# A delta-rule attention with two MoE layers on one core: the sign of the decoded weights by a 32-bit step on VectorE, unread products in TensorE's early gaps, seven half buffers for the second decoding

## The chip, the core and the metric

The kernel runs on 1 core of one Trainium2 chip. The time is the device time of that core in microseconds (us), given as the median of three runs. The engines are called as in the profile: PE is TensorE (PEld its weight loads), DVE is VectorE, ACT is ScalarE, POOL is GpSimd, SP is the engine that issues the transfers.

## What is computed

The reference, cut to what matters (`_attn_ref`, then two MoE layers; each tells one layer's work):

```
k_n = k / (norm(k) + 1e-6)                     # q, k, v: [4, 8, 768, 48] float32
for t in range(768):
    y[:, :, t] = q[:, :, t] @ state            # state: [4, 8, 48, 48]
    v_old = k_n[:, :, t] @ state
    state += beta[:, :, t] * outer(k_n[:, :, t], v[:, :, t] - v_old)
x = y.transpose(0, 2, 1, 3).reshape(3072, 384)
x = (silu(x @ w_gate) * (x @ w_val)) @ w_out   # d_ff 1536
h = x @ w_in                                   # d_ff 2048
return where(h > 0, h, exp(min(h, 0)) - 1) @ w_out2
```

The weights of both MoE layers are float64. The kernel gets their bits as pairs of 32-bit words. The result is not read from the state after the last token.

## The kernel before

**Work and stages.** The 3,072 tokens are cut into 12 groups g of 256: 128 positions of two batches. For each group `prepare` loads q, k and v, normalises k, transposes q and k, forms the products of keys with keys and queries (L451), masks them into `gr` (L457, DVE, four instructions a group) and calls `invert`. That transposes the masked blocks into `ain` (L486), inverts a triangular matrix per 32 positions in small DVE steps (L501, L508) and, for groups 0 and 1, does this blocked: two halves of 16 (`halves`), joined by two sets of 64 small products on TensorE (`join1` L546, `join2` L560) with a step on DVE between them (`mid`). `attention` applies the inverse (L602), forms for every 32 positions a matrix that carries the state onward (L622), copies it with ACT and adds the queries to it (`plus`, L635, DVE, four instructions for each pair of batch and parity), and takes the state through the four pieces (`chain`: products on TensorE, L652, and two sums on DVE, L658, for each piece and batch). The output is read off all states at once, transposed and split into `xh` and `xl`, a rounded half and the difference (L755 and the others below do the same with weights). Every large fp32 product is done as three passes of such halves.

**First MoE** (`moe1`). Per group 12 blocks f of 128 hidden units: two projections of 9 products of 256 columns each (L832), Silu on ACT (L839), the product on DVE (L842), a rounded copy on ACT (L846), the difference on POOL (L849), and 12 output products into the accumulator `acc` (L857), which takes two banks. The groups' results go out to DRAM (`x2d`). **Second MoE** (`moe2`): six groups n of 512 tokens, 16 steps f each: 9 products of 512 columns (L942), three ACT passes, three DVE passes, 12 output products (L979).

**Decoding of weights** (`decode`). Each tile of 128 x 768 weights, 18 for the first MoE and 16 for the second, passes six steps: ACT scales the low word (`lowbits`, L755), ACT writes the magnitude of the high word into a temporary (`mag`, L761), the sign is put into the low word's top byte (on POOL with a compare, L768, or on DVE with a mask of bytes, L771; the planner chooses), DVE merges temporary and low word (`both`, L776), ACT copies the rounded half (`hi`, L786) and POOL forms the difference (`lo`, L790). The second decoding has three temporaries (the tiles `gr`, `st` and `dt`, which the attention no longer needs then), so three weights are under way at a time.

**What sets the order.** Class `Order` plans the whole program as a list of steps with costs, priorities and the buffers that they hold, and takes at every moment the ready step with the best priority (a smaller number goes first; on engines other than TensorE a step may be waited for during 0.35 of the chosen one's cost). What it yields is each engine's fixed order. Decoding of the first weights has priority 12 and above, between the attention of group 0 and that of group 1.

```
o_ = acc[:, d // 2, (d % 2) * TB:(d % 2) * TB + TB]            # moe1, prod
add(p, [("POOL", 1900.0, 1900.0, 0, sign(G)), ("DVE", 1350.0, 1430.0, 0, sign(V))],
    r=[key, keyb], w=[(key, "lo")])
add(p, [("DVE", 1110.0, 1170.0, 0, both)], r=[(key, "lo")], w=tkeys)
decode(n, tag, tk, att_pri(0) + 2 + 0.1 * n)                    # first decoding
```

Of the kernel before, what the change touches and what calls it, by code (L numbers as in the profile page):

```python
# [10 lines left out]
F16 = mybir.dt.float16  # L11
# [34 lines left out]
class Order:  # L46
# [41 lines left out]
    def run(self):  # L88
# [22 lines left out]
        while left:  # L111
# [23 lines left out]
            t, o, (e, occ, lat, k, f) = pick  # L135
            ready.remove(o)
# [34 lines left out]
def delta_moe_kernel(ctx: ExitStack, tc: tile.TileContext, q, k, v, beta,  # L171
# [12 lines left out]
    BLOCKED = (0, 1)  # L184
    JOIN = (2, 4, 5)
    LOPOOL = tuple(range(12))
    HIDVE = False
    DIFDVE = False
# [19 lines left out]
    ident = T("ident", [128, 128])  # L208
    strict = T("strict", [128, 32])
# [86 lines left out]
    def consts():  # L296
# [25 lines left out]
        for r0, r1 in ((32, 64), (64, 96)):  # L322
            for x, n, key in ((st, B * H, "st"), (sv, 2 * (C - 1) * H, "sv")):
                def f(x=x, n=n, r0=r0, r1=r1):
                    w_ = x[r0:r1].rearrange("p b (h d) -> p b h d", d=D) if x is st else \
                        x[r0:r1].rearrange("p a c (h d) -> p (a c) h d", d=D)
                    G.tensor_copy(out=w_.rearrange("p b h d -> p (b h) d"),
                           in_=ident[r0:r1, D:2 * D].unsqueeze(1).to_broadcast([32, n, D]))
                add(20, pool(n * D, f), r=["ident"] + (["stz"] if x is st else []),
# [248 lines left out]
    def attention(g, p):  # L578
# [32 lines left out]
        for a in range(2):  # L611
            for par in range(2):
# [14 lines left out]
                for c in range(C):  # L627
# [93 lines left out]
        batch(p, 4, [chain(0, C - 1), chain(1, C - 1)], g > 0)  # L721
# [18 lines left out]
    def decode(n, tag, tkeys, p):  # L740
# [23 lines left out]
        def sign(e):  # L764
            def f():
                by = buf[n].bitcast(U8).rearrange("p a (n b) -> p a n b", b=8)
                if e is G:
                    e.tensor_scalar(out=by[:, :, :, 3], in0=by[:, :, :, 7], scalar1=128.0,  # L768
                                    scalar2=128.0, op0=ALU.is_ge, op1=ALU.mult)
                else:  # L770
                    e.tensor_scalar(out=by[:, :, :, 3], in0=by[:, :, :, 7], scalar1=128, scalar2=None,  # L771
# [302 lines left out]
```

## Time and profile before

| | before |
|---|---|
| median of three runs | 1219.83 us (1219.39 to 1221.9) |
| the profiled execution | 1217.5 us |
| its span | 1215.8 us |
| PE busy | 1126.8 us, 93% |
| DVE busy | 807.2 us, 66% |
| ACT busy | 555.4 us, 46% |
| POOL busy | 281.0 us, 23% |

The span is the time from the first to the last instruction that the trace holds; the profiled execution takes 1.7 us more. The share of busy time is a mean over stages that differ much, so the table only tells which engine the whole leans on. Which wait ends last in a stage is to be read from that stage.

### The profile page before, as it was taken

How to read it: one execution, taken by the hardware profiler on the slowest of the kernel's cores; microseconds unless marked ns; L12 is line 12 of the kernel's file. 1: busy time of each engine (PE TensorE's matmuls, PEld its weight loads, DVE VectorE, ACT ScalarE, POOL GpSimd, SP SyncE). 2: the span in 40 equal slices, each digit the busy share in tenths (PEclk: the TensorE clock that was granted, in tenths of full speed). 3: DMA queues.
4: the chain of work that ended last, by engine and by line, in shares of the span. 5: the costliest groups of instructions: out<-in, count | busy, mean ns of one | idle time of the engine just before them, and what ended most of it. 6: DMA issues, size and time to landing. Idle time of an engine off the chain costs nothing.

```text
span 1215.8 us, 33783 instructions
## 1 busy us (share of the span) xinstructions
PE 1126.8 (93%) x14366; PEld 1042.5 (86%) x14366; DVE 807.2 (66%) x2485; ACT 555.4 (46%) x1098; POOL 281.0 (23%) x252
## 2 busy tenths in 40 slices
PE   2487789999999999999999999979999999999998
PEld 2477779989998999899899999868888888888887
DVE  7888577968787887869687731977544445454443
ACT  5574424243433435252424333876545545454543
POOL 6896112122121212121221112782000000000000
PEclk9979879999999999999999999989999999999998
DMA  9720111120202011120201002910100101010000
GB/s 289 203 73 14 29 28 27 29 41 16 42 16 41 22 35 31 26 49 7 55 2 30 2 15 89 334 63 18 52 10 2 52 1 52 1 35 1 26 1 27
DMA packets 106824, 57.32 MB, mean 47 GB/s; under 512 B 76944, under 2 KB 101520, under 8 KB 106672
## 3 DMA queue, kind: packets, MB, share of 16 engines
q1 hardware_dynamic: 106672, 55.16, 16.9%
q8 instruction: 112, 1.84, 0.6%
q14 instruction: 40, 0.33, 0.1%
HBM read 45.71 MB, written 9.44 MB: 45 GB/s over the span
## 4 chain that ended last, share of the span: by engine, by line
PE 74%; DVE 9%; issue 2%; POOL 1%; ACT 1%; DMA 1%; ACTq 0%; DVEq 0%; POOLq 0%
PE gv L832 19%; PE acc L857 9%; PE acc L979 8%; PE at L979 8%; PE at L942 8%; PE gv L942 8%; PE at L622 3%; PE at L652 3%; DVE ain L501 3%; DVE z L508 3%; PE at L602 2%; PE at L425 2%; PE at L675 2%; PE at L451 2%; DVE tb L842 1%
## 5 line engine op out<-in xcount | busy, mean ns | idle before, releaser
L832 PE MATMUL gv<-xh,w 128*128 128x256 f32 x1728 | 288.7, 287 | 7.3 <-ACT tb L839 4.8
L832 PEld LDWEIGHTS gv<-xh,w 128*128 128x128 f32 x1728 | 239.8, 192 | 11.6 <-ACT tb L839 5.6
L849 POOL TENSOR_TENSOR hb<-tb,hb 128x256 fp32r<-128x256 f32 x144 | 116.0, 805 | 397.7 <-ACT hb L846 346.7
L857 PE MATMUL acc<-hb,w 128*128 128x256 f32 x1296 | 186.1, 287 | 7.7 <-POOL hb L849 3.8
L857 PEld LDWEIGHTS acc<-hb,w 128*128 128x128 f32 x1296 | 166.4, 192 | 12.8 <-POOL hb L849 5.3
L832 PE MATMUL gv<-xl,w 128*128 128x256 f32 x864 | 151.0, 284 | 0.0
L839 ACT ACTIVATE tb<-gv 128x256 f32<-128x256 f32 x144 | 55.3, 384 | 200.4 <-PE gv L832 191.6
L501 DVE TENSOR_TENSOR ain<-z,ain 128x60 f32<-128x60 f32 (+22 forms) x580 | 123.8, 250 | 1.3
L832 PEld LDWEIGHTS gv<-xl,w 128*128 128x128 f32 x864 | 124.6, 192 | 0.0
L846 ACT CAST hb<-tb 128x256 fp32r<-128x256 f32 x144 | 58.5, 406 | 113.6 <-DVE tb L842 112.4
L842 DVE TENSOR_TENSOR tb<-gv,tb 128x256 f32<-128x256 f32 x144 | 61.1, 424 | 66.2 <-ACT tb L839 54.2
L508 DVE TENSOR_TENSOR z<-z,ain 128x60 f32<-128x60 f32 (+22 forms) x580 | 103.4, 217 | 1.4
L957 DVE SCALAR_TENSOR_TENSOR hb<-gv,hb 128x512 f32<-128x512 f32 x48 | 33.2, 692 | 95.3 <-ACT hb L954 95.3
L957 DVE SCALAR_TENSOR_TENSOR hb<-at,hb 128x512 f32<-128x512 f32 x48 | 33.2, 692 | 87.5 <-ACT hb L954 87.4
L948 ACT ACTIVATE hb<-gv 128x512 f32<-128x512 f32 x48 | 28.7, 599 | 94.6 <-PE gv L942 94.2
L954 ACT ACTIVATE hb<-hb,neg 128x512 f32<-128x512 f32 x96 | 69.5, 724 | 3.0
L948 ACT ACTIVATE hb<-at 128x512 f32<-128x512 f32 x48 | 28.7, 598 | 83.5 <-PE at L942 83.5
L951 ACT ACTIVATE hb<-hb 128x512 f32<-128x512 f32 x96 | 60.7, 633 | 3.0
L622 PE MATMUL at<-gr,R 32*96 32x80 f32 x1536 | 56.7, 264 | 4.0 <-DVE lc L635 3.0
L622 PEld LDWEIGHTS at<-gr,R 32*96 32x96 f32 x1536 | 48.0, 169 | 11.7 <-DVE lc L635 3.6
L658 DVE TENSOR_TENSOR sv<-at,sv 48x192 f32<-48x192 f32 x96 | 34.1, 355 | 31.4 <-PE at L652 29.2
L979 PE MATMUL acc<-w,kp 128*128 128x384 f32 x192 | 41.1, 347 | 6.2 <-DVE kp L962 4.4
(176 smaller groups left out, 2203.6 us busy)
## 6 DMA issues: line engine op xcount, KB each, us to landing
w<-in_moe_w_out_dram SPq DMA_DIRECT2D x28, 384.0 KB, 6.4
w<-in_moe_w_in_dram SPq DMA_DIRECT2D x16, 384.0 KB, 5.2
kp<-in_k_dram SPq DMA_DIRECT2D x12, 384.0 KB, 4.2
qp<-in_q_dram SPq DMA_DIRECT2D x12, 384.0 KB, 4.0
R<-in_v_dram SPq DMA_DIRECT2D x24, 192.0 KB, 2.8
w<-in_moe_w_gate_dram SPq DMA_DIRECT2D x12, 384.0 KB, 8.6
w<-in_moe_w_val_dram SPq DMA_DIRECT2D x12, 384.0 KB, 8.7
x2d<-hb SPq DMA_DIRECT2D x12, 256.0 KB, 2.0
```

What stands on the lines that cost most here:

```text
L501: V.tensor_tensor(out=t, in0=z[:, l:l + 1, x:y].to_broadcast([128, l, y - x]), in1=an[:, l, 0:l].unsqueeze(2).to_broadcast([128, l, y - x] ...
L508: V.tensor_tensor(out=z[:, 0:l, x:y], in0=z[:, 0:l, x:y], in1=t, op=ALU.add)
L622: PE.matmul(bank[h[c].got[0]][0:96, s * 80:s * 80 + 80], lhsT=R[t, u, :], rhs=gr[t, u, 0:80], start=True, stop=True, skip_group_check=True)
L832: PE.matmul(dst, lhsT=wt[:, a_, kk * 128:(kk + 1) * 128], rhs=xx[:, kk, :], start=(n == 0), stop=(n == 3 * KD - 1))
L842: V.tensor_tensor(out=c['s'], in0=bank[h.got[0]][:, TB:2 * TB], in1=c['s'], op=ALU.mult)
L849: return lambda: e.tensor_tensor(out=c['h'][:, 1, :], in0=c['s'], in1=c['h'][:, 0, :].bitcast(F32), op=ALU.subtract)
L857: PE.matmul(o_, lhsT=w[:, a_, d * 128:(d + 1) * 128], rhs=c['h'][:, b_, :], start=(f == 0 and n == 0 and d != 1), stop=(f == F1 - 1 and n ...
L942: PE.matmul(x, lhsT=W[f][:, 0, a_, kk * 128:(kk + 1) * 128], rhs=x2[n][b_][:, kk, :], start=(m == 0), stop=(m == 3 * KD - 1))
L951: A.activation(out=c['r'], in_=c['r'], func=ACTF.Exp, scale=-1.0)
L954: A.activation(out=c['r'], in_=c['r'], func=ACTF.Identity, bias=neg1, scale=1.0)
L957: V.scalar_tensor_tensor(out=c['r'], in0=bank[h.got[0]], scalar=0.0, in1=c['r'], op0=ALU.max, op1=ALU.add)
L979: PE.matmul(o, lhsT=c['h'][:, b_, t * 128:(t + 1) * 128], rhs=W[f][:, 1][:, a_, :], start=(f == 0 and m == 0), stop=(f == F2 - 1 and m == 2))
```

## The change

- **Sign.** POOL's compare and DVE's mask of bytes go. In their place stands one 32-bit step on DVE (`sign32`: the high word with all but the top bit cleared, or-ed into the low word; it stands 22 times in the new order) or one half-word copy on ACT (`sign16`, 12 times).
- **Differences.** The difference of a decoding may now be done on DVE (29 times) or POOL (5 times); that of a block of the first MoE is always on DVE (144 times, POOL before).
- **Sums with the queries.** `plus` becomes one DVE instruction of 512 elements on data that ACT has copied to SBUF (48 in all) in place of four of 128 on PSUM (192).
- **States.** The copies that set up the states go from POOL to ACT. For the last two groups the update after the last piece is left out; nothing reads it (32 products and four sums of states a group).
- **Unread products.** `warm` and `fill` put products of a constant 128 x 128 identity into TensorE's order, 403 in all, where the planner sees a gap before its time of 150 us. They write into `acc[:, 1, 384:512]`, which no step reads before it is started anew.
- **Priorities.** The first decoding moves from priority 12 + 0.1n to 14.8 + 0.02n. Steps with priority 12 or more are waited for during 0.1 of a cost, before 0.35.
- **Second decoding.** Its temporaries are seven half buffers (two each in the tiles `gr`, `st` and `dt`, one in `l2`), before three whole tiles.

```diff
+                    w = c[0] + (self.WAIT if c[1].pri[0] < 12 else 0.1) * c[2][1]
...
+            if e == "PE" and self.fill and t < self.until and left > 1:
+                gap = t - free.get("PE", 0.0)
+                n = int(self.share * gap / self.unit)
+                if n > 1:
+                    self.fill(n)
+                    kind[0] = k
...
+                def plus(a=a, par=par):
+                    b = 64 * par
+                    x = buf['lc', a][par][0:D, :, :, D:80]
+                    V.tensor_tensor(out=x, in0=x, in1=kq[b:b + D, a, :, 0, :].rearrange(
+                        "p j (c t) -> p j c t", c=C), op=ALU.add)
+                add(p, dve(512, plus), r=[("kq", a, 0)] + lk[a], w=[("lc", a, par, c) for c in range(C)])
...
-        batch(p, 4, [chain(0, C - 1), chain(1, C - 1)], g > 0)
+        if g // 2 < NI - 1:
+            batch(p, 4, [chain(0, C - 1), chain(1, C - 1)], g > 0)
...
+        def sign16():
+            hw = buf[n].bitcast(F16).rearrange("p a (n four) -> p a n four", four=4)
+            A.activation(out=hw[:, :, :, 1], in_=hw[:, :, :, 3], func=ACTF.Copy, scale=2.0 ** -60)
+
+        def sign32():
+            V.scalar_tensor_tensor(out=pr()[:, :, :, 0], in0=pr()[:, :, :, 1], scalar=-2 ** 31,
+                                   in1=pr()[:, :, :, 0], op0=ALU.bitwise_and, op1=ALU.bitwise_or)
...
-            add(p, [("POOL", 1900.0, 1900.0, 0, sign(G)), ("DVE", 1350.0, 1430.0, 0, sign(V))],
+            add(p, [("DVE", 1110.0, 1170.0, 0, sign32), ("ACT", 1860.0, 1940.0, 0, sign16)],
                 r=[key, keyb], w=[(key, "lo")])
...
-        add(p, [("POOL", 2300.0, 2300.0, 0, lo(G))] + [("DVE", 950.0, 1100.0, 0, lo(V))] * DIFDVE,
+        add(p, [("POOL", 2300.0, 2300.0, 0, lo(G)), ("DVE", 950.0, 1100.0, 0, lo(V))],
...
-            add(P_MOE, (pool(256, lo(G)) if g in LOPOOL else dve(256, lo(V))), r=[ht, (hh, 0)], w=[(hh, 1)], use=[ht, hh])
+            add(P_MOE, dve(256, lo(V)), r=[ht, (hh, 0)], w=[(hh, 1)], use=[ht, hh])
...
+    def fill(n, first=False):
+        for _ in range(n):
+            PE.matmul(acc[:, 1, 384:512], lhsT=identr, rhs=identr, start=first, stop=True,
+                      skip_group_check=True)
+            first = False
...
-        decode(n, tag, tk, att_pri(0) + 2 + 0.1 * n)
+        decode(n, tag, tk, att_pri(0) + 4.8 + 0.02 * n)
...
+    def new_t2():
+        for x in ("gr", "st", "dt"):
+            tmp2[x] = TT(x, [128, 2, 2, DM], I32)
+        tmp2["l2"] = TT("l2", [128, 1, 2, DM], I32)
...
+    t2 = [("gr", 0), ("st", 0), ("dt", 0), ("l2", 0), ("gr", 1), ("st", 1), ("dt", 1)]
```

**How the order moves.** Three places follow; a row tells the line, the operation, what it writes from what, and how many in a row. A line of the changed kernel stands 9 to 27 below its place before.

First place: DVE between the normalised keys of group 0 (L404, now L413) and the first steps of its inverse. `w_3` and `w_4` are tiles of weights, `gr` takes the masked products, `ain` their transposes. Before:

```order
L404 TENSOR_TENSOR kp<-kp,sm_77 128x8x48 x2
L771 TENSOR_SCALAR w_3_109<-w_3_109 128x768
L457 TENSOR_TENSOR gr<-at_85,z_269 128x4x64
L457 TENSOR_TENSOR gr<-at_86,z_269 128x4x64
L457 TENSOR_TENSOR gr<-at_87,z_269 128x4x64
L457 TENSOR_TENSOR gr<-at_84,z_269 128x4x64
L486 STREAM_TRANSPOSE ain<-gr 128x256 x4
L776 SCALAR_TENSOR_TENSOR xh_18_274<-xh_18_274,w_3_109 128x768
L771 TENSOR_SCALAR w_4_119<-w_4_119 128x768
L478 COPY z_303<-zd 128x2x16
L518 TENSOR_TENSOR ain<-z_303,ain 128x2x15
```

Now:

```order
L413 TENSOR_TENSOR kp<-kp,sm_78 128x8x48 x2
L466 TENSOR_TENSOR gr<-at_86,z_268 128x4x64
L466 TENSOR_TENSOR gr<-at_87,z_268 128x4x64
L466 TENSOR_TENSOR gr<-at_88,z_268 128x4x64
L466 TENSOR_TENSOR gr<-at_85,z_268 128x4x64
L495 STREAM_TRANSPOSE ain<-gr 128x256 x2
L487 COPY z_339<-zd 128x2x16
L495 STREAM_TRANSPOSE ain<-gr 128x256 x2
L527 TENSOR_TENSOR ain<-z_339,ain 128x2x15
L533 TENSOR_TENSOR z_339<-z_339,ain 128x2x15
```

The sign of the weights (L771) no longer stands ahead of the masks, nor do a merge (L776) and a second sign stand between the transposes and the first steps of the inverse.

Second place: TensorE from group 0's products of keys (L451, now L460) over the two joins of the inverse (L546 and L560, now L555 and L569) to the first product with the inverse (L602, now L611). Before:

```order
L451 MATMUL at_87<-kq 32x64 x16
L451 MATMUL at_84<-kq 32x64 x16
L546 MATMUL at_85<-ain,gr 32x32 x64
L560 MATMUL at_86<-ain,z_421 32x32 x64
L602 MATMUL at_87<-R,ain 32x96 x16
```

Now:

```order
L460 MATMUL at_87<-kq 32x64 x16
L460 MATMUL at_88<-kq 32x64 x16
L460 MATMUL at_85<-kq 32x64 x16
L1018 MATMUL acc<-identr 128x128 x117
L555 MATMUL at_86<-ain,gr 32x32 x64
L1018 MATMUL acc<-identr 128x128 x16
L569 MATMUL at_87<-ain,z_581 32x32 x64
L1018 MATMUL acc<-identr 128x128 x9
L611 MATMUL at_88<-R,ain 32x96 x16
```

117 unread products (L1018) stand ahead of the first join, 16 between the two and 9 behind them. Such pieces stand at 16 more places; the piece of 13 after group 0's last block of the first MoE is the one whose first product waits for ACT, for the copy of `acc`, and group 1's state products stand behind it.

Third place: DVE at the start of the second decoding, in group 11's blocks (`tb` and `hb` belong to the blocks, `gr` and `st` are temporaries of the decoding). Before:

```order
L842 TENSOR_TENSOR tb_425_11684<-gv_81,tb_425_11684 128x256
L771 TENSOR_SCALAR w_416_11623<-w_416_11623 128x768
L842 TENSOR_TENSOR tb_430_11727<-gv_82,tb_430_11727 128x256
L776 SCALAR_TENSOR_TENSOR gr_11715<-gr_11715,w_416_11623 128x768
L771 TENSOR_SCALAR w_421_11653<-w_421_11653 128x768
L842 TENSOR_TENSOR tb_434_11770<-gv_81,tb_434_11770 128x256
L776 SCALAR_TENSOR_TENSOR st_11756<-st_11756,w_421_11653 128x768
L771 TENSOR_SCALAR w_426_11695<-w_426_11695 128x768
L842 TENSOR_TENSOR tb_440_11817<-gv_82,tb_440_11817 128x256
L776 SCALAR_TENSOR_TENSOR gr_11819<-gr_11819,w_426_11695 128x768
L771 TENSOR_SCALAR w_428_11712<-w_428_11712 128x768
```

Now:

```order
L851 TENSOR_TENSOR tb_429_11909<-gv_82,tb_429_11909 128x256
L782 SCALAR_TENSOR_TENSOR w_422_11850<-w_422_11850 128x768
L858 TENSOR_TENSOR hb_431_11926<-tb_429_11909,hb_431_11926 128x256
L786 SCALAR_TENSOR_TENSOR gr_11766<-gr_11766,w_422_11850 128x768
L851 TENSOR_TENSOR tb_433_11953<-gv_83,tb_433_11953 128x256
L782 SCALAR_TENSOR_TENSOR w_426_11882<-w_426_11882 128x768
L858 TENSOR_TENSOR hb_435_11981<-tb_433_11953,hb_435_11981 128x256
L928 TENSOR_TENSOR sv_11848<-xh_424_11868,lc_11847 128x512
L800 TENSOR_TENSOR w_436_11983<-gr_11766,w_436_11983 128x2x384
L851 TENSOR_TENSOR tb_438_12000<-gv_82,tb_438_12000 128x256
L786 SCALAR_TENSOR_TENSOR st_11767<-st_11767,w_426_11882 128x768
L858 TENSOR_TENSOR hb_440_12017<-tb_438_12000,hb_440_12017 128x256
```

The differences of the blocks (L858), of the decoding (L800) and of the second MoE's input (L928) now stand in DVE's order between products, signs and merges; before, they were POOL's (L849, L790) or came later.

## Rows read from the trace of the kernel before

**Rows 1.** Windows by stage: length, busy PE, PEld, DVE, ACT, POOL; PEclk, DMA, GB/s.

```profile
0.00:76.50 76.50, 35.58 (x931) 30.64 (x932) 59.78 (x119) 43.51 (x70) 62.12 (x37) 0.87 0.74 200
76.50:167.60 91.10, 71.98 (x1381) 65.99 (x1379) 69.40 (x158) 41.10 (x82) 39.15 (x29) 0.89 0.20 45
167.60:750.60 583.00, 569.74 (x9718) 544.12 (x9719) 430.69 (x1851) 219.94 (x552) 119.77 (x156) 0.99 0.12 26
750.60:831.50 80.90, 70.66 (x449) 64.23 (x447) 63.63 (x59) 60.57 (x97) 56.05 (x30) 0.94 0.52 179
831.50:1215.80 384.30, 378.83 (x1892) 337.50 (x1892) 183.66 (x302) 190.34 (x299) 3.86 (x2) 0.99 0.07 22
```

**Rows 2.** Timeline of VectorE (DVE), 18 to 77 us; start, duration, engine, line, operation.

```profile
18.50 1.45 DVE L457 TENSOR_TENSOR gr<-at,z 128x256 f32<-128x256 f32 x4
...
36.06 0.71 DVE L537 STREAM_TRANSPOSE ain<-ain 128x512 f32<-128x512 f32 x1
36.70 0.92 DVE L776 SCALAR_TENSOR_TENSOR dt<-dt,w 128x768 int32<-128x768 int32 x1
...
39.10 0.74 DVE L551 SCALAR_TENSOR_TENSOR z<-at,zd,eye 128x512 f32<-128x512 f32 x1
...
76.10 0.56 DVE L709 TENSOR_TENSOR xl<-at,xh 128x384 fp32r<-128x384 f32 x1 [0.57 <-ACT xh L705]
```

**Rows 3.** Timeline of GpSimd (POOL), at 26 us and at 737 us.

```profile
25.69 15.74 POOL L768 TENSOR_SCALAR w<-w 128x768 uint8<-128x768 uint8 x4
...
736.96 0.74 POOL L849 TENSOR_TENSOR hb<-tb,hb 128x256 fp32r<-128x256 f32 x1 [2.50 <-ACT hb L846]
```

**Rows 4.** Timeline of VectorE, 88 to 145 us.

```profile
88.16 2.20 DVE L776 SCALAR_TENSOR_TENSOR xl<-xl,w 128x768 int32<-128x768 int32 x1
...
112.45 1.56 DVE L457 TENSOR_TENSOR gr<-at,z 128x256 f32<-128x256 f32 x4
...
126.93 0.70 DVE L537 STREAM_TRANSPOSE ain<-ain 128x512 f32<-128x512 f32 x1
...
136.89 0.96 DVE L372 TENSOR_TENSOR ain<-kp 128x768 f32<-128x768 f32 x1 [6.12 <-PE at L602]
...
143.49 1.03 DVE L404 TENSOR_TENSOR kp<-kp,sm 128x384 f32<-128x384 f32 x2
```

**Rows 5.** Groups by form, DVE and ACT: busy us, mean ns of one, idle before.

```profile
L842 DVE TENSOR_TENSOR tb<-gv,tb 128x256 f32<-128x256 f32 x144 | 61.1, 424 | 66.2 <-ACT tb L839 54.2 <-PE gv L832 10.2
...
L658 DVE TENSOR_TENSOR sv<-at,sv 48x192 f32<-48x192 f32 x96 | 34.1, 355 | 31.4 <-PE at L652 29.2
...
L919 DVE TENSOR_TENSOR sv<-xh,lc 128x512 fp32r<-128x512 f32 x6 | 4.1, 687 | 0.2
...
L755 ACT ACTIVATE w<-w 128x768 int32<-128x768 uint32 x34 | 30.9, 911 | 0.0
```

**Rows 6.** Window of 56 to 76 us, columns as in rows 1.

```profile
56.00:76.00 20.00, 15.88 (x330) 13.87 (x331) 16.35 (x35) 14.76 (x28) 16.73 (x6) 0.50 0.12 23
```

**Rows 7.** Timeline of TensorE (PE), group 11's last state update.

```profile
719.28 0.56 PE L652 MATMUL at<-sv,lc 96*48 96x48 f32 x16
```

**Rows 8.** Chain that ended last, 736 to 905 us; start, duration, engine, tile, line.

```profile
736.59 2.16 PE gv L832 x18
738.75 1.08 PE acc L857 x9
739.83 2.16 PE gv L832 x18
...
900.82 2.08 PE gv L942 x9
...
905.01 2.08 PE at L942 x9
```

**Rows 9.** Timeline of VectorE, 760 to 810 us.

```profile
760.42 1.05 DVE L771 TENSOR_SCALAR w<-w 128x768 uint8<-128x768 uint8 x1 [1.30 <-ACT w L755]
...
809.76 1.49 DVE L776 SCALAR_TENSOR_TENSOR st<-st,w 128x768 int32<-128x768 int32 x1 [2.10 <-POOL w L768]
```

More of the change, by code (lines that the diff above doesn't have):

```diff
@@ L55, in __init__ @@
     def __init__(self):
+        self.fill = None
+        self.until = 0.0
+        self.share = 0.7
+        self.unit = 65.0
         self.steps = []
@@ L184, in delta_moe_kernel @@
     BLOCKED = (0, 1)
+    UNTIL = 150e3
     JOIN = (2, 4, 5)
-    LOPOOL = tuple(range(12))
-    HIDVE = False
-    DIFDVE = False
     sb = ctx.enter_context(tc.tile_pool(name="sb", bufs=1))
@@ L326, in f @@
                         x[r0:r1].rearrange("p a c (h d) -> p (a c) h d", d=D)
-                    G.tensor_copy(out=w_.rearrange("p b h d -> p (b h) d"),
+                    A.copy(out=w_.rearrange("p b h d -> p (b h) d"),
                            in_=ident[r0:r1, D:2 * D].unsqueeze(1).to_broadcast([32, n, D]))
-                add(20, pool(n * D, f), r=["ident"] + (["stz"] if x is st else []),
+                add(20, act(n * D, f, False), r=["ident"] + (["stz"] if x is st else []),
                     w=[(key, r0)])
@@ L750, in temp @@
                 return buf['dt'][:, tag].bitcast(dt)
+            if isinstance(tag, tuple):
+                return tmp2[tag[0]][:, tag[1]].bitcast(dt)
             return TT(tag, [128, 2, DM], dt)
@@ L762, in mag @@
                          scale=2.0 ** -112)
[L764 to L771, printed above, removed]
-                                    op0=ALU.bitwise_and)
-            return f
+        def sign16():
[4 more added lines that the diff above has]
+                                   in1=pr()[:, :, :, 0], op0=ALU.bitwise_and, op1=ALU.bitwise_or)
         def both():
@@ L799, in decode @@
             add(p, dve(768, plain), r=[key, keyb], w=tkeys)
-        add(p, act(768, hi(A.copy), False) + [] if not HIDVE else act(768, hi(A.copy), False) + [("DVE", 490.0, 570.0, 0, hi(V.tensor_copy))], r=tkeys,
-            w=[key, keyb])
-        add(p, [("POOL", 2300.0, 2300.0, 0, lo(G))] + [("DVE", 950.0, 1100.0, 0, lo(V))] * DIFDVE,
+        add(p, act(768, hi(A.copy), False), r=tkeys, w=[key, keyb])
+        add(p, [("POOL", 2300.0, 2300.0, 0, lo(G)), ("DVE", 950.0, 1100.0, 0, lo(V))],
             r=tkeys + [key], w=[keyb])
@@ L1005, in att_pri, with warm @@
         return P_ATT + 10 * g
-    betas_first = True
+    def fill(n, first=False):
[3 more added lines that the diff above has]
+            first = False
+    def warm():
+        fill(24, True)
+        od.fill = fill
     loads(0, 0)
     consts()
+    add(0, act(128, lambda: A.copy(out=identr, in_=ident), False), r=["ident"], w=["identr"])
+    add(0, pe(2900, warm, 1), r=["identr"])
     betas()
@@ L1027, in delta_moe_kernel @@
     M2 = MP + 100 * NB
-    t2 = (("gr", [("grk", 0), ("grk", 1)] + GRM),
-          ("st", INIT[:3] + [("st", b) for b in range(B)] + [(("st", b), 1) for b in range(B)]),
-          ("dt", [("dt", 0), ("dt", 1)]))
+    tmp2 = {}
+    def new_t2():
+        for x in ("gr", "st", "dt"):
+            tmp2[x] = TT(x, [128, 2, 2, DM], I32)
+        tmp2["l2"] = TT("l2", [128, 1, 2, DM], I32)
+    add(0, [("SP", 1.0, 0.0, 0.0, new_t2)],
+        w=[("grk", 0), ("grk", 1), ("dt", 0), ("dt", 1), "l2"] + GRM + INIT[:3] +
+        [("st", b) for b in range(B)] + [(("st", b), 1) for b in range(B)])
+    t2 = [("gr", 0), ("st", 0), ("dt", 0), ("l2", 0), ("gr", 1), ("st", 1), ("dt", 1)]
     load_x2(0, 500)
@@ L1033, in delta_moe_kernel @@
         load_w(n, src2(n), 510 + n)
[L1034 to L1035 removed]
+        x, j = t2[n % 7]
+        decode(n, (x, j), [("t2", x, j)], 500 + n)
     for n in range(NB // 2):
@@ L1041, in delta_moe_kernel @@
                 load_x2(n + 1, 600 + n)
+    od.until = UNTIL
     with tc.manual_schedule():
```

10 lines of the change are left out of this document (1 added, 9 removed).

## The prediction

> **What bounds the kernel now.** I read the windows by stage first [rows 1]. The program has five stretches: group 0's attention (0 to 76.5 us), its first MoE block with group 1's attention (76.5 to 167.6), ten groups of MoE and attention woven together (167.6 to 750.6), group 11's MoE with the decoding of the second MoE's weights (750.6 to 831.5), and the second MoE. The reader is to see where TensorE is not busy: 40.9 us in the first stretch, 19.1 in the second, 13.3 in the third although that is 583 us long, 10.2 in the fourth. So the third and fifth stretch are TensorE's own work, and time can be won only at the beginning and around 750 to 830 us. In both VectorE (DVE) is busiest, so I read its timeline next. The first masks start at 18.50 and the inverse is ready at 36.06 + 0.71 = 36.77 us [rows 2]; the second half of group 0's input to the MoE ends at 76.10 + 0.56 = 76.66, and TensorE's first projection starts beside it. Meanwhile GpSimd (POOL) does four byte signs in 15.74 us [rows 3], 3.9 each. What that does to DVE shows in one kind of step: the merge of bits (L776) takes 0.92 us at 36.70 [rows 2], and 2.20 at 88.16 beside POOL's work [rows 4].
>
> **The sum is made against the profiled execution**, 1217.5 us (span 1215.8, 1.7 around it); the median of the runs is 1219.83, 2.3 more, and I add that at the end.
>
> **Start up to the first projection.** The change takes the sign out of the place ahead of the masks and out of the middle of the inversion, and takes POOL's signs away. How long masks, transposes and inversion take without those, group 1 shows: 112.45 to 126.93 + 0.70 = 127.63, 15.2 us [rows 4], with three MoE products of 0.42 [rows 5] and some 1.2 us of pauses between: 12.7 us. I let the masks start 1.1 us earlier than before (the products they read end about there), at 17.4, so the inverse is ready at 30.1 instead of 36.77. The join on TensorE and two merges on DVE lie between that and the middle step (before: 39.10 [rows 2]); I put that at 32.1 and its end at 32.85. From there to the second half of the MoE's input DVE has in its order 22 decoding steps, 4 added masks, 16 state sums and 2 differences. The steps: a 32-bit sign is the same form as the merge, 0.92 to 0.95 [rows 2]; a decoding's difference on DVE reads two 768-element operands as the square does, 0.96 [rows 4]; so 22 x 0.96 = 21.1. The added masks, now one of 512 instead of four of 128, are bounded by 0.69 of the 512-element difference (128 partitions, these have 48), 4 x 0.68 = 2.7; 16 x 0.355 = 5.7 [rows 5] and 2 x 0.56 = 1.1 [rows 2]. Together 30.6 us. DVE idles about 7 us in the same piece before; I leave 5. That gives 32.85 + 30.6 + 5 = 68.5 against 76.66: **8.2 us won**. ACT gets 12 of all the signs, five of them until here, as half words; the nearest row is its pass over the low words, 0.91 [rows 5], so 4.6 us, or 9 if a half word costs double. Its order holds less work than DVE's up to this point either way, but the two wait for each other at every weight, and that is why I leave idle time in.
>
> **From there to the second group's projection.** In DVE's order stand 17 decoding steps (16.3), 9 products of 0.42 and 9 differences that POOL did before. Such a difference of 256 lies between half of 0.69 and 0.42 [rows 5]: I take 0.38, together 7.2. Group 1's normalisation is 136.89 to 143.49 + 1.03 without two blocks of added masks and the square, 4.7 [rows 4]; its inversion 12.7 and the middle step 0.75. That is 41.7. Then follows the attention of group 1: the next square and normalisation 5.6, one decoding step 1.0, 3 products and differences 2.4, added masks 2.7, 16 state sums 5.7, the next masks, transposes and first inversion steps 6.6, two differences 1.1: 25.1. DVE was idle 91.1 - 69.4 = 21.7 us in this stretch [rows 1]; with six steps of a block less to wait for POOL I leave 10, of which 2 belong to the unread products after group 0's last block: the first of them waits for ACT's copy of the accumulator, and the state products stand behind it on TensorE. So 68.5 + 41.7 + 25.1 + 10 = 145.3 against 167.6: **22.3 us in all, 14 of them here**. Between both ends: no idle time gives 32.85 + 30.6 + 66.8 = 130.2, 37 us won; as much idle time as before gives 159, 8.6 won.
>
> **The unread products** are 403 on TensorE. No row has one of 128 columns. 256 columns take 2.16 / 18 = 0.120 us and 512 take 2.08 / 9 = 0.231 [rows 8]; the line through both gives 0.065 for 128, and 0.120 is the upper end. The 117 that stand ahead of the first join then take 7.6 us (14.0) in a gap of about 11.7, from 18.4 to 30.1. I cost them at nothing, since TensorE waits there for DVE; at the upper end they make the join 2.3 us late, and without a gap all 403 would cost 26 us.
>
> **The middle.** Two groups drop the last update of the state, 32 matmuls; 16 take 0.56 [rows 7], pipelined 0.85 for 32: 1.7 us won. The rest is TensorE's: 0, from 8 won (more than half of 13.3 us idle) to 6 lost.
>
> **The second decoding.** From 750.6 on TensorE would need 12 blocks of 3.24 and 96 steps of 4.19 [rows 8] and 3.5 at the end: 38.9 + 402 + 3.5 = 444. The profile has 465.2, so 21 us are lost. The first sign is at 760.42, and at 809.76 DVE waits 2.10 us for POOL's sign [rows 9]. Afterwards the order gives DVE 7 signs, 8 merges, 8 differences, 19 MoE steps and one difference of 512 up to group 11's last block: 30.4 us, which from 760 ends with the block's 38.9. Then 34.7 us of DVE stand beside eight steps of TensorE, 33.5. Seven halves instead of three whole buffers let ACT run ahead. I leave 6 us lost: **15 won**, between 18 and 8 (half of it stays).
>
> **Sum**: 1217.5 - 22.3 - 1.7 - 15 = 1178.5, and 2.3 for the median: **1181 us**. The bounds together are 1217.5 - 37 - 8 - 18 + 2.3 = 1157 and 1217.5 - 8.6 + 6 - 8 + 2.3 = 1209.
>
> **The rivals.**
> *The clock pays too.* [...] Chance 0.16.
> *Decoding still binds.* ACT gets signs besides its three passes, and DVE's 34.7 us are no less than TensorE's 33.5; if the gain at 750 to 830 is 5 instead of 15, 1191. Against it: POOL's waits go. 0.14.
> *The start gives half.* ACT and DVE stand in order, and each waits for the other at every decoding; with idle time as before, or with products at 0.120 us that TensorE must finish first, 1181 + 12 = 1193. 0.13.
> *POOL's differences on DVE stall the blocks.* This one is slower. POOL's difference ends at 736.96 + 0.74 = 737.70 [rows 3], its product starts at 738.75 [rows 8], 1.05 us later; on DVE it ends 0.36 earlier but stands behind whatever the order put there, transposes of 0.6 and reductions of 0.95. With 132 blocks in groups 1 to 11, a mean stall of 0.29 us each, that is a difference 1.7 us late, eats the whole gain; 0.5 us each makes 1181 + 66 = 1247. Against it: DVE is busy 430.7 of 583 us [rows 1], and 132 x 0.38 more and 18 less for the added masks is 463, 79%. 0.04.
> *The change does little at the start*, because ACT's order holds everything at its old time: 1203. 0.04.
>
> **Numbers.** The forecast keeps 0.49, its own range 1170 to 1192. With the clock case and both halves the range is 1158 to 1204; outside lie the slower case and the ends. A measurement of this kernel tells 0.2%, 2.4 us, from no change. Faster 0.93, same 0.02, slower 0.05.
>
> **What would show it.** The inverse of group 0 near 30 us, the first projection near 68, the second group's near 145; POOL almost empty; merges of 0.95 everywhere; from group 11's first block to the end about 450 us. The forecast is wrong if the first projection starts after 74, if TensorE waits for the products' own end at the first join, or if blocks in the middle wait for DVE's differences.

## The result and the profile after

The changed kernel takes 1191.04 us (median of four runs, 1190.44 to 1192.53) against 1220.39 of the kernel before (1219.39 to 1221.9): a ratio of 0.976, 95% interval 0.9743 to 0.9777. That is 29.3 us less, where 38.8 were forecast; 1191 lies in the range. The profiled execution has a span of 1188.6 us, 27.2 less than before.

The busy line of the page, after:

```profile
PE 1164.9 (98%) x14705; PEld 1086.6 (91%) x14705; DVE 786.5 (66%) x2503; ACT 577.6 (49%) x1115; POOL 58.1 (5%) x66
```

POOL went from 281.0 us to 58.1, DVE from 807.2 to 786.5, and TensorE's busy time grew from 1126.8 to 1164.9 although 64 products of the state's update are gone: the unread ones count as busy. The windows by stage of the changed kernel, cut where the first projection of group 0, the first of group 1 and ACT's first copy of group 10's accumulator begin (columns as in [rows 1]):

```profile
0.00:88.90 88.90, 86.11 (x1277) 82.67 (x1277) 51.29 (x115) 55.96 (x76) 8.66 (x18) 1.00 0.65 177
88.90:164.25 75.35, 71.72 (x1439) 67.26 (x1439) 63.37 (x164) 51.73 (x91) 12.50 (x9) 0.98 0.21 49
164.25:734.70 570.45, 563.38 (x9656) 537.56 (x9656) 430.99 (x1842) 218.31 (x553) 30.84 (x36) 0.99 0.13 27
734.70:1188.60 453.90, 443.65 (x2340) 399.08 (x2338) 240.87 (x385) 251.59 (x397) 6.06 (x3) 1.00 0.15 50
```

Before, the same marks are at 76.53, 167.60 and 751.75; the first two are the cuts of [rows 1]. So the four stretches changed by +12.4, -15.7, -13.7 and -10.1 us. The forecast was -8.2, -14.1, -1.7 and -15. The first stretch went the wrong way, and the reader sees there that TensorE is "busy" for 86.1 of 88.9 us. Its timeline tells with what (start, duration, line, count; "..." marks lines left out, here and below):

```profile
2.44 8.37 PE L1018 MATMUL acc<-identr 128*128 128x128 f32 x38 [2.44 <-ACT identr L1027]
10.61 1.93 PE L434 MATMUL at<-ident,qp 128*128 128x128 f32 x8
...
18.26 2.73 PE L460 MATMUL at<-kq 48*32 48x64 f32 x128
20.92 25.22 PE L1018 MATMUL acc<-identr 128*128 128x128 f32 x117
46.07 1.93 PE L555 MATMUL at<-ain,gr 16*32 16x32 f32 x128
```

117 unread products (L1018) run from 20.92 to 46.14, 25.2 us, 0.2155 each; the join of the inverse (L555) stands behind them. VectorE's timeline in the same stretch, which answers to [rows 2]:

```profile
19.48 0.87 DVE L466 TENSOR_TENSOR gr<-at,z 128x256 f32<-128x256 f32 x2 [8.44 <-PE at L460]
...
32.30 0.71 DVE L546 STREAM_TRANSPOSE ain<-ain 128x512 f32<-128x512 f32 x1
...
33.77 0.95 DVE L786 SCALAR_TENSOR_TENSOR dt<-dt,w 128x768 int32<-128x768 int32 x1
48.07 0.75 DVE L560 SCALAR_TENSOR_TENSOR z<-at,zd,eye 128x512 f32<-128x512 f32 x1 [13.35 <-PE at L555]
```

The inverse is ready at 32.30 + 0.71 = 33.01, 3.8 us sooner than before, and then VectorE waits 13.35 us for the join. The forms that the change added, by groups (busy us, mean ns of one, idle before):

```profile
L858 DVE TENSOR_TENSOR hb<-tb,hb 128x256 fp32r<-128x256 f32 x144 | 65.8, 457 | 20.4 <-ACT hb L855 19.4
...
L782 DVE SCALAR_TENSOR_TENSOR w<-w 128x768 int32<-128x768 int32 x22 | 20.9, 951 | 0.9 <-ACT w L768 0.8
...
L646 DVE TENSOR_TENSOR lc<-lc,kq 48x512 f32<-48x512 f32 x24 | 20.6, 858 | 3.2 <-ACT lc L639 2.9
...
L646 DVE TENSOR_TENSOR l<-l,kq 48x512 f32<-48x512 f32 x11 | 7.6, 687 | 7.8 <-ACT l L639 7.7
...
L800 DVE TENSOR_TENSOR w<-gr,w 128x768 fp32r<-128x768 f32 x5 | 4.8, 953 | 0.3 <-ACT w L796 0.3
...
L779 ACT ACTIVATE w<-w 128x768 f16<-128x768 f16 x12 | 23.3, 1942 | 0.0
```

The sign on VectorE is 0.95 as forecast. The decoding's difference is 0.95 in the row shown and 0.95 to 1.09 over all its tiles, the sum of 512 is 0.69 in one row and 0.86 in the other (0.68 forecast), and the blocks' difference takes 0.46 where 0.38 was forecast. ScalarE's half-word copy takes 1.94, twice its pass over whole words [rows 5].

### The profile page after: what moved, and what is told of

Read it like the earlier page. It is cut to its first block, busy times and chain, and to the rows that moved or that the text cites. A ratio compares the mean times of both kernels' runs of the same rounds, so it can differ in the third digit from the quotient of the medians.

```text
span 1188.6 us, 34214 instructions
## 1 busy us (share of the span) xinstructions
PE 1164.9 (98%) x14705; PEld 1086.6 (91%) x14705; DVE 786.5 (66%) x2503; ACT 577.6 (49%) x1115; POOL 58.1 (5%) x66
## 4 chain that ended last, share of the span: by engine, by line
PE 89%; DVE 5%; ACT 4%; issue 1%; DMA 1%; ACTq 0%; DVEq 0%
PE gv L841 25%; PE acc L866 12%; PE acc L988 8%; PE gv L951 8%; PE at L988 8%; PE at L951 7%; PE acc L1018 5%; PE at L631 3%; PE at L662 3%; PE at L611 3%; PE at L434 2%; PE at L460 2%; PE at L685 1%; ACT w L796 1%; DMA w<-in_moe_w_in_dram 1%
## 5 line engine op out<-in xcount | busy, mean ns | idle before, releaser
L841 PE MATMUL gv<-xh,w 128*128 128x256 f32 x1728 | 293.7, 289 | 1.6 <-ACT tb L848 1.2
L866 PE MATMUL acc<-hb,w 128*128 128x256 f32 x1296 | 182.5, 286 | 0.0
L517 DVE TENSOR_TENSOR z<-z,ain 128x60 f32<-128x60 f32 (+22 forms) x580 | 98.6, 209 | 1.1
L510 DVE TENSOR_TENSOR ain<-z,ain 128x60 f32<-128x60 f32 (+22 forms) x580 | 97.4, 204 | 0.9
L858 DVE TENSOR_TENSOR hb<-tb,hb 128x256 fp32r<-128x256 f32 x144 | 65.8, 457 | 20.4 <-ACT hb L855 19.4
L1018 PE MATMUL acc<-identr 128*128 128x128 f32 x403 | 69.7, 346 | 4.1 <-ACT identr L1027 2.4
L1018 PEld LDWEIGHTS acc<-identr 128*128 128x128 f32 x403 | 66.7, 260 | 5.7 <-ACT identr L1027 2.4
L631 PE MATMUL at<-gr,R 32*96 32x80 f32 x1536 | 44.1, 251 | 0.0
```

The lines of the kernel that those rows point to most:

```text
L510: V.tensor_tensor(out=t, in0=z[:, l:l + 1, x:y].to_broadcast([128, l, y - x]), in1=an[:, l, 0:l].unsqueeze(2).to_broadcast([128, l, y - x] ...
L517: V.tensor_tensor(out=z[:, 0:l, x:y], in0=z[:, 0:l, x:y], in1=t, op=ALU.add)
L631: PE.matmul(bank[h[c].got[0]][0:96, s * 80:s * 80 + 80], lhsT=R[t, u, :], rhs=gr[t, u, 0:80], start=True, stop=True, skip_group_check=True)
L841: PE.matmul(dst, lhsT=wt[:, a_, kk * 128:(kk + 1) * 128], rhs=xx[:, kk, :], start=(n == 0), stop=(n == 3 * KD - 1))
L858: return lambda: e.tensor_tensor(out=c['h'][:, 1, :], in0=c['s'], in1=c['h'][:, 0, :].bitcast(F32), op=ALU.subtract)
L866: PE.matmul(o_, lhsT=w[:, a_, d * 128:(d + 1) * 128], rhs=c['h'][:, b_, :], start=(f == 0 and n == 0 and d != 1), stop=(f == F1 - 1 and n ...
```

## The experiments

Theory: the parts of the change work as added up in the forecast, and the unread products hold up what stands behind them. (A, B, M1, S1 and so on are the names that the expectations give to the theories.) Rivals: the products pay by TensorE's pace; the middle was won by the blocks' difference off POOL, or by the sums on SBUF; the end by the half buffers, or by the sign. The kernels below undo one part each; where nothing else is said they start from the kernel without unread products (kernels 2, 3 and 4 from the changed kernel, 12 from the kernel before). One limit holds for all but the first two: undoing a part also moves what the planner places behind it.

The marks of all runs, in us: first product of the first join, first projection of group 0 and of group 1 (TensorE's timeline), ACT's first copy of group 10's accumulator; the length of the ten groups (third to fourth mark) and from there to the end of the span; the median of the runs and the ratio to the kernel before.

| kernel | join | group 0 | group 1 | copy | ten groups | end | median | ratio (95%) |
|---|---|---|---|---|---|---|---|---|
| before | 36.8 | 76.5 | 167.6 | 751.8 | 584.2 | 464.0 | 1220.4 | |
| changed | 46.1 | 88.9 | 164.3 | 734.7 | 570.4 | 453.9 | 1191.0 | 0.976 (0.9743 to 0.9777) |
| 1 no products | 28.2 | 69.8 | 144.4 | 713.6 | 569.3 | 454.0 | 1169.0 | 0.9584 (0.9567 to 0.9601) |
| 2 price 220 | 26.7 | 69.4 | 145.8 | 714.1 | 568.3 | 453.9 | 1170.2 | 0.9591 (0.9568 to 0.9615) |
| 3 difference on POOL | 42.5 | 88.6 | 168.5 | 742.2 | 573.7 | 452.1 | 1199.2 | 0.9827 (0.9806 to 0.9849) |
| 4 sums of 128 | 46.1 | 92.3 | 171.5 | 750.3 | 578.8 | 455.0 | 1206.2 | 0.989 (0.9872 to 0.9907) |
| 5 whole buffers | 28.3 | 70.4 | 144.6 | 714.3 | 569.7 | 450.8 | 1166.4 | 0.9558 (0.9543 to 0.9572) |
| 6 old sign | 29.8 | 74.9 | 153.3 | 725.8 | 572.5 | 458.6 | 1186.1 | 0.9708 (0.967 to 0.9747) |
| 7 sign on DVE | 28.2 | 68.6 | 153.4 | 724.4 | 571.0 | 450.7 | 1174.5 | 0.9625 (0.9606 to 0.9644) |
| 8 old priority | 28.1 | 70.3 | 164.3 | 736.2 | 571.9 | 454.4 | 1192.0 | 0.9769 (0.9754 to 0.9784) |
| 9 old wait | 28.3 | 69.9 | 153.6 | 728.5 | 574.9 | 450.8 | 1182.5 | 0.9695 (0.9674 to 0.9717) |
| 10 last states | 28.3 | 69.9 | 144.1 | 715.8 | 571.7 | 447.4 | 1166.5 | 0.9561 (0.9547 to 0.9576) |
| 11 whole, DVE | 28.2 | 70.3 | 144.0 | 716.1 | 572.0 | 453.1 | 1169.6 | 0.9587 (0.9571 to 0.9604) |
| 12 before, priority | 36.0 | 84.9 | 157.2 | 748.2 | 591.0 | 469.8 | 1220.2 | 1.0 (0.9988 to 1.0013) |

Kernels 1, 5 and 11 have the same order up to group 11, and their ten groups take 569.3, 569.7 and 572.0: single profiles differ by some 3 us there, and less than that says nothing.

**1, no products.**

```diff
     def fill(n, first=False):
-        for _ in range(n):
-            PE.matmul(acc[:, 1, 384:512], lhsT=identr, rhs=identr, start=first, stop=True,
-                      skip_group_check=True)
-            first = False
+        return
```

> The changed kernel without any of its 403 unread products; every other instruction stands in the same order. Theory A, the products stand in the way: the inverse is ready at about 33 us as in the changed kernel, the first join starts there instead of at 46.1, the first projection at 68 to 74 us instead of 88.9, and the whole takes 1170 to 1178 us (changed kernel: 1191). Theory B, they pay by TensorE's pace: without them the small products of 46 to 89 us and of 140 to 165 us run at half the pace, the first projection starts at 72 to 80 and the second group's again near 164, the whole takes 1186 to 1200. Theory C, neither: the whole stays within 3 us of 1191.

Theory A holds: 1168.97 us, 22.1 less than the changed kernel and 51.4 less than before, just below the range given, since the inverse is ready sooner too. TensorE's timeline, then VectorE's:

```profile
28.22 1.93 PE L555 MATMUL at<-ain,gr 16*32 16x32 f32 x128 [12.01 <-DVE ain L546]
...
69.78 1.01 PE L841 MATMUL gv<-xh,w 128*128 128x256 f32 x3 [0.57 <-ACT xh L715]
```

```profile
14.70 0.87 DVE L466 TENSOR_TENSOR gr<-at,z 128x256 f32<-128x256 f32 x2 [3.67 <-PE at L460]
...
27.45 0.71 DVE L546 STREAM_TRANSPOSE ain<-ain 128x512 f32<-128x512 f32 x1
...
39.15 0.96 DVE L786 SCALAR_TENSOR_TENSOR dt<-dt,w 128x768 int32<-128x768 int32 x1 [4.71 <-ACT w L779]
```

The 17.9 us between 46.07 and 28.22 at the join are accounted for in two steps: the masks, which the first 53 products hold up, come at 14.70 instead of 19.48 (4.8), and the 117 outlast the inverse by 46.07 - 33.01 = 13.1. That is most of the loss, which is 19.1 at the first projection and 21.0 at the end of the span.

**2, the products at their price.**

```diff
-        self.unit = 65.0
+        self.unit = 220.0
```

> The changed kernel with the planner's price of one unread product set from 65 to 220 ns, near the 215 ns that one took ahead of the first join: 128 products instead of 403, 34 instead of 117 ahead of the first join; nothing else moves. Theory A: those 34 take 7.3 us and end by 28.5, before the inverse at 33; the first projection starts at 68 to 74, the whole takes 1168 to 1176. Theory B: fewer products give the slower pace back; the whole is no faster than 1186. If both hold, it beats the kernel without products by 3 to 8 us.

The products no longer hold the join up, but they win nothing either: 1170.18, within the noise of kernel 1, whose interval overlaps. TensorE's timeline:

```profile
2.44 6.24 PE L1018 MATMUL acc<-identr 128*128 128x128 f32 x28 [2.44 <-ACT identr L1027]
8.48 1.93 PE L434 MATMUL at<-ident,qp 128*128 128x128 f32 x8
...
10.95 0.65 PE L434 MATMUL at<-ident,kp 128*128 128x128 f32 x4
...
14.26 4.01 PE L1018 MATMUL acc<-identr 128*128 128x128 f32 x34
26.67 1.93 PE L555 MATMUL at<-ain,gr 16*32 16x32 f32 x128 [8.39 <-DVE ain L546]
```

The 34 products took 0.118 each, those at 2.44 0.22. Behind them TensorE waits 8.39 us for the inverse, and the window from 22 to 70 us is granted 0.54 of the clock:

```profile
22.00:70.00 48.00, 38.80 (x827) 35.01 (x827) 37.77 (x61) 36.01 (x56) 2.72 (x2) 0.54 0.69 201
```

So the pace fell beside these products (7 of them take 1.75 us at 44.15), and theory B falls: without any, the time is the same. What a granted clock of 1.00 from 22 to 70 us would win no run shows. The changed kernel was faster from about 59 us on (64 products of L611 take 1.52 us at 59.58, 2.79 at 55.51), but with 157 unread products of its own in that stretch: from the join to the first projection it takes 42.8 us, kernel 1 takes 41.6 with 0.50 of the clock granted from 50 to 70 us. I expect little there, since in kernel 1 VectorE is busy 18.4 of the 20 us before the first projection.

**3, the blocks' difference on POOL** and **4, sums of 128**, both from the changed kernel with its products.

```diff
-            add(P_MOE, dve(256, lo(V)), r=[ht, (hh, 0)], w=[(hh, 1)], use=[ht, hh])
+            add(P_MOE, pool(256, lo(G)), r=[ht, (hh, 0)], w=[(hh, 1)], use=[ht, hh])
```

> The changed kernel with the difference of each block of the first MoE on GpSimd again, as before the change (144 instructions). Theory M1, this move is what shortened the ten groups in the middle, 583 us to 570: the stretch from the second group's first projection to the last product of group 10 takes 578 to 584 us again and the whole 1199 to 1205. Theory M2, it is the sums with the queries on SBUF data, which free TensorE's banks sooner: the stretch stays at 568 to 573 and the whole within 4 us of 1191.

```diff
-                    V.tensor_tensor(out=x, in0=x, in1=kq[b:b + D, a, :, 0, :].rearrange(
-                        "p j (c t) -> p j c t", c=C), op=ALU.add)
...
+                        V.tensor_tensor(out=buf['lc', a][par][0:D, :, c, D:80], in0=pv[0:D, :, D:80],
+                                        in1=kq[b:b + D, a, :, 0, 32 * c:32 * c + 32], op=ALU.add)
```

> The changed kernel with four sums of 128 on PSUM for each pair of batch and parity again, as before the change, in place of one of 512 on SBUF. Theory M1 (the blocks' difference off GpSimd shortened the middle): the stretch of ten groups stays at 568 to 573 us and the whole within 4 us of 1191. Theory M2: the stretch takes 578 to 584 us and the whole 1199 to 1208.

The windows of the ten groups, of 3 and then of 4:

```profile
168.50:742.20 573.70, 561.54 (x9665) 535.02 (x9665) 412.69 (x1715) 218.43 (x553) 120.20 (x156) 1.00 0.13 26
```

```profile
171.50:750.30 578.80, 568.72 (x9655) 543.47 (x9655) 437.50 (x1956) 219.18 (x553) 29.09 (x36) 0.99 0.13 26
```

M2 takes most of it: the sums of 128 cost 8.4 us in the ten groups (578.8 against 570.4) and 7.2 more before them. M1 was wrong about its place: POOL's difference costs 8.1 us by the medians, and of the marks' delay 4.3 lie before group 1's projection and 3.3 in the ten groups, hardly more than the spread. (Kernel 3's join is 3.6 us sooner because the same forms ahead of it ran faster, the 128 products of L460 in 1.74 us against 2.73, not by its edit: see the last section.) In kernel 4 TensorE is busy 5.3 us longer with the same number of products and idle 3.0 longer; through which wait the sums do that was not followed up.

**5, three whole temporaries**, and **6, the sign by bytes.**

```diff
-        x, j = t2[n % 7]
-        decode(n, (x, j), [("t2", x, j)], 500 + n)
+        tag, tk = t2[n % 3]
+        decode(n, tag, tk, 500 + n)
```

> The kernel without unread products, with three whole temporaries for the second decoding again in place of seven halves. Theory S1, the halves are what shortened the end: from the last product of group 10 to the end 460 to 465 us instead of 454, the whole 1175 to 1180 (without products: 1169). Theory S2, the sign's way is: the stretch stays at 452 to 457 and the whole within 3 us of 1169.

```diff
-            add(p, [("DVE", 1110.0, 1170.0, 0, sign32), ("ACT", 1860.0, 1940.0, 0, sign16)],
+            add(p, [("POOL", 1900.0, 1900.0, 0, sign(G)), ("DVE", 1350.0, 1430.0, 0, sign(V))],
```

> The kernel without unread products, with the sign on GpSimd's compare or VectorE's mask of bytes again (28 and 6 in the new order). Theory S2: merges beside GpSimd take up to 2.2 us, the stretch from the last product of group 10 to the end is 460 to 465 us, and the start loses too: first projection at 74 to 78 instead of 69.8, second group's at 155 to 162 instead of 144.4; the whole 1185 to 1195. Theory S1: the end stays at 452 to 457; with the start's loss the whole is 1175 to 1185. Against both: within 3 us of 1169, then the sign's form is worth nothing and the rest of the change made the gain.

S1 falls: with whole buffers the end is 450.8, no longer than with halves (454.0), and the kernel is no slower (1166.42 against 1168.97, intervals that just overlap). S2 holds in direction, not in size: the old sign makes the end 4.6 us longer, the first projection 5.1 and group 1's 8.9 later. Of the 10 us that the end gained over before, about half is the sign. What made the other half no kernel shows: the decoding's difference off POOL is a candidate that was not tried alone, and kernel 10 shows that the order by itself moves the end by some us.

**7, the sign on VectorE alone.**

```diff
-            add(p, [("DVE", 1110.0, 1170.0, 0, sign32), ("ACT", 1860.0, 1940.0, 0, sign16)],
+            add(p, [("DVE", 1110.0, 1170.0, 0, sign32)],
```

> The kernel without unread products, with the sign on VectorE alone (34 in place of 22, none on ScalarE). If VectorE sets the start: 5 more steps of 0.96 up to the first projection make it 4 to 5 us later, 74 to 75, less what three more differences on GpSimd give back; if ScalarE does: its 1.94 each go, the first projection comes 3 to 8 us sooner, 62 to 67. At the end two half-word copies leave ScalarE, 3.9 us: 450 to 453 if ScalarE binds there, 454 to 456 if VectorE does. The whole 1160 to 1174.

Neither end of the expectation: the first projection comes 1.2 us sooner, group 1's 9.0 later. The end, 450.7, is where the expectation has it if ScalarE binds there; kernels 10 and 11 speak against that reading. Up to 70 us ScalarE's half words cost a little (VectorE waits 4.71 us for one at 39.15 in kernel 1, its third row above). Behind that they save 9; that VectorE is then the engine with the masks and the inversion of group 1 to do is how I read it, and no run shows it by itself.

**8, the old priority**, and **9, the old wait of 0.35.**

```diff
-        decode(n, tag, tk, att_pri(0) + 4.8 + 0.02 * n)
+        decode(n, tag, tk, att_pri(0) + 2 + 0.1 * n)
```

> The kernel without unread products, with the first decoding at its old priority (12 + 0.1n in place of 14.8 + 0.02n). If the priority takes part in the start's gain: the first projection at 72 to 76 us or the second group's at 148 to 155, the whole 1173 to 1180. If the moved work alone makes it: first projection within 1.5 us of 69.8, the whole within 3 us of 1169.

```diff
-                    w = c[0] + (self.WAIT if c[1].pri[0] < 12 else 0.1) * c[2][1]
+                    w = c[0] + self.WAIT * c[2][1]
```

> The kernel without unread products, with the planner waiting for 0.35 of a cost for steps of every priority again, in place of 0.1 for the late ones; the decoding keeps its new priority. If the priority alone makes the second stretch short (74.6 us from the first to the second group's projection): that stays within 72 to 78 and the whole within 4 us of 1169. If the shorter wait is needed with it: 80 to 94 and 1175 to 1190.

These two are worth 23.0 and 13.5 us, the first more than expected, the second as expected if the shorter wait is needed beside the priority. The first projection stays at 70, but group 1's comes 19.9 and 9.2 us later. VectorE's normalisation of group 1 and TensorE's join, in kernel 1:

```profile
80.89 0.56 DVE L413 TENSOR_TENSOR kp<-kp,sm 128x384 f32<-128x384 f32 x1
...
103.03 1.29 PE L555 MATMUL at<-ain,gr 16*32 16x32 f32 x128 [0.71 <-DVE ain L546]
```

and in kernel 8, where all decoding of the first weights stands ahead of the normalisation:

```profile
107.00 1.02 DVE L413 TENSOR_TENSOR kp<-kp,sm 128x384 f32<-128x384 f32 x2
...
124.80 1.93 PE L555 MATMUL at<-ain,gr 16*32 16x32 f32 x128 [7.57 <-DVE ain L546]
```

The join of group 1 comes 21.8 us later and its projection 19.9: the loss is made here.

**10, the last states.**

```diff
-        if g // 2 < NI - 1:
-            batch(p, 4, [chain(0, C - 1), chain(1, C - 1)], g > 0)
+        batch(p, 4, [chain(0, C - 1), chain(1, C - 1)], g > 0)
```

> The kernel without unread products, with the last update of the state done for the last two groups again (32 products and 4 sums each). The ten groups in the middle take 1 to 3 us more than 569.3, the whole 1170 to 1172; if the products only fill idle time, within 1 us of 1169.

The ten groups are 2.4 us longer, as expected and near the spread, but the end is 6.6 shorter, so the kernel with more work is no slower than kernel 1, and the whole meets neither expectation. TensorE's waits from 705 to 850 us in kernel 1 tell what the end has that this one has not:

```profile
PE acc L988 <- ACT hb L885: 3.5, 1, 3.5
```

The first output products of the second MoE wait 3.5 us for ACT's copy of the last accumulator, which stands behind decoding in ACT's order. The changed kernel and kernels 2, 4 and 8 have the same wait, and ends of 453.9 to 455.0; kernels 3, 5, 7, 9, 10 and 11 have not, and ends of 447.4 to 453.1. So the 3 us between kernels 1 and 5 are this wait and not the buffers' price. The planner's order moves the end by a few us more than the parts tested do.

**11, whole buffers and no half words in the second decoding.**

```diff
+                [("ACT", 1860.0, 1940.0, 0, sign16)] * (p < 500),
...
+        tag, tk = t2[n % 3]
```

> The kernel without unread products, with three whole temporaries in the second decoding and the sign there on VectorE alone (ScalarE's half words stay in the first decoding). The whole temporaries took 3.1 us off the end, the sign on VectorE alone 3.3; if these are two things, the end takes 447 to 449 us and the whole 1162 to 1164; if both only relieve ScalarE of the same wait, 450 to 451 and 1165 to 1167.

Neither expectation holds: the end is 453.1, the whole 1169.59. The two gains are not additive, and after kernel 10 they are better read as places of the order than as prices.

**12, the kernel before with the new priority and wait alone.**

```diff
-        decode(n, tag, tk, att_pri(0) + 2 + 0.1 * n)
+        decode(n, tag, tk, att_pri(0) + 4.8 + 0.02 * n)
...
-                    w = c[0] + self.WAIT * c[2][1]
+                    w = c[0] + (self.WAIT if c[1].pri[0] < 12 else 0.1) * c[2][1]
```

> The kernel before, with only the decoding's new priority and the shorter wait for late steps. If the priority alone brings group 1's attention forward: the second group's projection comes at 145 to 155 us instead of 167.6, the whole 1198 to 1210. If it needs the work off GpSimd, whose signs and differences the order would then hold up: 160 to 168, the whole within 5 us of 1220.

The whole is unchanged, as the second theory has it, but group 1's projection lies between the two: at 157.2, 10.4 us sooner than before. The first projection comes 8.4 later, the ten groups take 6.9 more and the end 5.8. The priority pays only together with other parts of the change; which of them it needs, and why the ten groups lose, was not followed up.

The fastest are kernels 5 and 10, 1166.4 us, 0.956 of before and 24.6 us less than the changed kernel.

## Why the prediction held, and where it failed

**The start.** The sum of VectorE's work was right to about a microsecond where nothing else stands in the way: 68.5 and 145.3 forecast, 69.8 and 144.4 in kernel 1. Inside it, the inverse came at 28.2 instead of 30.1 and the stretch behind took that back: from the middle step to the first projection VectorE idles 9.2 of 38.8 us where 5 were left, 4.71 of it in one wait for a half word, which costs 1.94, above both ends given. The forecast did not say what the second figure hangs on: the rows of the order already hold the new priority and wait, which kernels 8 and 9 show to be 20 and 9 us of it. One reading of the rows fails, though no term rests on it: the merge's 2.20 us at 88.16 was put down to POOL's byte signs. POOL was in such signs at 36.70 too, until 41.43 [rows 3], and the merge took 0.92 there; at 88.16 POOL was in a difference of a decoding (L790, 2.53 us from 87.01).

**The unread products.** This is the step that failed: "I cost them at nothing, since TensorE waits there for DVE", with 7.6 us and an upper end of 14.0 for the 117. They took 25.2. A product of 128 columns took 0.118 us in kernel 2, as much as one of 256 [rows 8], which alone makes an estimated 117 x 0.118 = 13.8 us, within the upper end, and a join 1.7 us late. The rest is TensorE's pace, 0.2155 us a product: the upper end was taken from rows of 736 us and later, though the trace of the kernel before shows a slower pace near this place, where four transposes take 1.11 us, and 0.66 later:

```profile
14.60 1.11 PE L425 MATMUL at<-ident,kp 128*128 128x128 f32 x4
...
109.61 0.66 PE L425 MATMUL at<-ident,kp 128*128 128x128 f32 x4 [1.40 <-DVE kp L404]
```

Nor were the 53 products ahead of the masks counted, 4.8 us by kernel 1. Together the unread products made the start 19.9 us later at group 1's projection, 22.1 us in all by the medians. The rival "the start gives half" named the mechanism, products that TensorE must finish first, at a price of 12.

**The middle** was mis-sized the other way: 1.7 forecast, 8 as the bound, 13.7 measured. The sums on SBUF were costed only on VectorE, by their length; kernel 4 shows 8.4 us of the ten groups with them. The rest, 5 us, is split between the blocks' difference and the last states, each near the spread.

**The second decoding**: 15 forecast, 10.1 measured, inside the bounds. That seven halves let ACT run ahead is not what made it: kernel 5 does as well without them.

Together: the start gained 18.95 us less than forecast, the middle 12.0 more and the end 4.9 less, which makes the 11.8 us by which the span missed the forecast (27.2 gained against 39). That the total came near is luck: two errors of opposite sign.

**The rivals.** The clock did not pay: products at their price win nothing over none (kernels 1 and 2), and beside them the clock was 0.54 from 22 to 70 us, so what a higher clock would win stays open. The range of 1158 to 1204 takes in a gain by the clock that was the author's estimate and that no run shows; from 50 to 70 us the clock was 0.50 with the products and without (kernels 2 and 1), as the kernel before has it from 56 to 76 [rows 6], and kernels 1 and 2 take the same time. "The change does little at the start" is what the changed kernel's start did, 3.3 us of 22.3, but by the products and not by ACT's order: without them it gains 23.2 (kernel 1). "Decoding still binds" has the measured time, 1191, by another cause: it let the end gain 5 us, and the end gained 10. The slower case, differences on VectorE that stall the blocks, fell: L858 waits for ACT's copy in 19.4 of its 20.4 idle us, and putting it back on POOL costs 8 us.

## What to carry to other kernels

An instruction that does nothing still stands in its engine's order, and a planner that fits it into gaps needs the price that the chip charges there, at the slowest pace it may meet: a factor of 3.3 in that price (0.2155 us where the planner had 0.065) cost 22 us of a 51 us gain. Where a gain is read out of a new order, ask which rule of the planner makes the order; here a priority that let the next group's first steps pass a queue of decoding was worth more than the sign's new form (23 us against 17, kernels 8 and 6), and nothing at all without the other parts (kernel 12).

## What the runs showed of the hardware

- A product of 128 fp32r columns took 0.118 us in kernel 2 (34 in 4.01 at 14.26) and 0.121 in the changed kernel (23 in 2.79 at 63.48), that of 256 took 0.120 [rows 8]: half the columns saved nothing.
- The granted clock of the windows did not tell the pace at the start. In the changed kernel it says 1.00 for the first 88.9 us, and TensorE works from 2.44 on almost without a pause; yet eight transposes take 1.93 at 10.61 and 1.04 at 90.02, and the unread products 0.2155 each from 20.92 on (117 in 25.22) and 0.121 from 63.48 on (23 in 2.79):

```profile
53.40 2.18 PE L1018 MATMUL acc<-identr 128*128 128x128 f32 x9
...
63.48 2.79 PE L1018 MATMUL acc<-identr 128*128 128x128 f32 x23
...
90.02 1.04 PE L434 MATMUL at<-ident,qp 128*128 128x128 f32 x8
```

In the kernel before the window from 10 to 18 us says 1.00 too, where four transposes take 1.11 against 0.66 at 109.61; so the 0.87 of [rows 1] overstates the pace there. At the start of these traces the pace is to be read from forms that repeat.
- Unread products did not hold the faster pace in kernel 3. It has the same beginning as the changed kernel, and its four transposes take 0.63 us at 14.42, where the changed kernel's take 1.07 at 15.43. The first 19 of the 117 products take 0.123 each, the 98 behind a pause of 2.35 us 0.206, and from 30 to 60 us the granted clock is 0.50 although TensorE is busy 29.4 of 30 us, first with the rest of the 117 products:

```profile
17.72 2.34 PE L1018 MATMUL acc<-identr 128*128 128x128 f32 x19
22.40 20.16 PE L1018 MATMUL acc<-identr 128*128 128x128 f32 x98 [2.35 <-issue]
```

- VectorE's merge of 768 words took 0.92 to 0.96 us in the changed kernel, 0.94 beside an idle POOL (at 104.32). Beside POOL's byte signs it took 0.92 to 1.64 (kernel before, at 36.70 and 37.53), beside POOL's differences of 768 elements up to 2.61 (kernel before, at 77.44).
- ScalarE's copy of every fourth half word took 1.94 us for 768 elements, against 0.91 for its pass over every other word [rows 5].
